# w_in cast to bf16 by the GpSimd queue's DMAs, VectorE's first step put in TensorE's order, and the last two blocks as whole-array matmuls

## The chip, the cores and the metric

The kernel runs on one core of one Trainium2 chip. The metric is the device time of one execution in microseconds (us). Nine executions of the kernel before gave a median of 699.18 us (698.62 to 701.48). Step and line numbers below are those of the kernel before; "u" is the index 0 to 15 of a tile of 128 columns of the hidden layer, "s" the index 0 to 31 of a step.

## The reference

`x` is [8, 4096, 192] float32. A causal convolution over the sequence with 7 taps comes first; the taps are the softmax of `weight` [8, 7] and each of the 8 heads owns 24 channels. The result, seen as 32768 tokens of 192 channels, goes through a feed-forward layer:

```python
h = x @ w_in                                  # [32768,192] @ [192,2048]
g = h * (1.0 / (1.0 + np.exp(-beta * h)))     # beta: one value for each of the 2048 columns
return (g @ w_out).astype(np.float32)         # [32768,2048] @ [2048,192]
```

## The kernel before, in words

The work is cut into 32 steps of 2 x 512 tokens: the same 512 positions of sequences p and p+4 (index h = 0, 1). The 192 channels are split as 64 partitions x 3 (index j or c), and the two values of h lie on partitions 0 to 63 and 64 to 127. So all of `w_in` is held twice as bf16, once on each half of the partitions (tile `w_in_s`, [128, 3, 2048]).

A step does this for each u:

- `hidden` (L405 to L424): six 64-row matmuls, three for each half, which run in pairs on the two halves of the array, into one of two PSUM buffers `ph`; then ScalarE's Silu (L421) from `ph` into `g`. It computes beta*h*sigmoid(beta*h), and `w_out` is divided by beta row by row in turn (`scale_w_out`, L305, four quarters on VectorE).
- `output` (L490): a number of "pairs". One pair is two 64-row matmuls of 192 columns (L443), on the two halves of the contraction, into the two rows of a PSUM tile `pa` or `pb`. A `Job` is two blocks of 128 tokens and takes 32 pairs; four jobs make a step's 128. When a job is done, `leave` (L454) adds the two rows on VectorE (L462) and SP stores the block. The last two jobs of the last step hold one block each (16 pairs); for those ScalarE copies one row (L459) and VectorE adds the other (L460). A job can take u only once u-2 of its own step is activated (LAG = 2), and steps 1 to 31 issue 8 pairs per u; step 0 issues 53 in all, so 75 pairs are always carried over into the next step.

The convolution of step s+2 is VectorE's work during step s and s+1: one multiply (L395) and six multiply-adds (L397) over [128, 1536] bf16, drawn from `queue`, one for each odd u (the "pops", L545). Its input is loaded two or three steps ahead (L95, SP), cast to bf16 (L106) and transposed by DMA (L127, SP).

The program writes out the order of every engine by hand (`manual_schedule`); each engine runs its own list in order. The start differs from a steady step:

- Step 0's tokens `x0` are cast (L241), transposed on TensorE (L248), copied by ScalarE (L290), and convolved on TensorE with seven diagonal matrices for each of c = 0, 1, 2 (L279). The three results leave PSUM by VectorE (L321, c = 0, 1) and ScalarE (L323, c = 2).
- `beta` is loaded by SP (L169) behind x0 and one half of w_in, and is transposed by a TensorE matmul (L331) that stands between the taps of c = 1 and those of c = 2.
- The first quarter of w_in (512 columns, u = 0 to 3) is loaded as float32 to both halves, one by SP (L168) and one by ScalarE's queue (L219), and cast by ScalarE (L301).
- Quarters 1 to 3 are cast by DMAs from GpSimd's queue (L208) to partitions 0 to 63 only; a small GpSimd copy (`hold`, L326) keeps them back until c = 0 is convolved. VectorE copies each to the other half (`copy_w_in`, L212, at u = 3, 5 and 9).
- Step 1's tokens `x1` are transposed on TensorE in `second` (u = 1 to 3). Its convolution is split: c = 0 on TensorE (`conv1`, taps 0 to 3 at u = 4 and 4 to 6 at u = 6, out of PSUM by VectorE, L381), c = 1, 2 on VectorE (seven operations over 1024 elements, L395 and L397, popped at u in 4, 6, 8, 9, 11, 12, 13).
- `fill` (L229) issues matmuls on zeros ahead of the first work.

SP issues its DMAs in this order: x0 (2), half of w_in's first quarter, beta, x1 (2), w_out (4), x of steps 2 and 3 (4), then transposes and stores.

Of the kernel before, what the change touches and what calls it, by code (L numbers as in the profile page):

```python
# [9 lines left out]
FP32 = mybir.dt.float32  # L10
FP32R = mybir.dt.float32r
BF16 = mybir.dt.bfloat16
AF = mybir.ActivationFunctionType
ALU = mybir.AluOpType
# [3 lines left out]
def kernel(  # L18
# [17 lines left out]
    nc = tc.nc  # L36

    B, S, D = x.shape
    H, K = weight.shape
    F = moe_w_in.shape[1]  # L40
    group = D // H
    DG = 64
    NG = D // DG
# [11 lines left out]
    N_ST = N_CH  # L55
# [6 lines left out]
    setup = ctx.enter_context(tc.tile_pool(name="setup", bufs=1))  # L62
# [70 lines left out]
    NW = 4  # L133
    FW = F // NW
# [3 lines left out]
    x0b = setup.tile([128, NB, NG, 2, DG], BF16)  # L138
    x1b = setup.tile([128, NB, NG, 2, DG], BF16)
    w_in_s = consts.tile([128, NG, F], BF16)  # L140
    w_in_raw = setup.tile([128, NG, FW], FP32)
    w_out_s = consts.tile([128, NF, D], BF16)
    w_out_raw = setup.tile([128, NF, D], FP32)
    w_in_v = moe_w_in.rearrange("(p c) f -> p c f", c=NG)
# [7 lines left out]
    cw8 = setup.tile([H, K], FP32)  # L152
    beta_q = setup.tile([NF, 128], FP32)
    nc.scalar.dma_start(out=cw8, in_=weight)


    def load_x(dst, t0):
# [7 lines left out]
            )  # L165

    load_x(x0, 0)
    nc.sync.dma_start(out=w_in_raw[0:DG], in_=w_in_v[:, :, 0:FW])  # L168
    nc.sync.dma_start(out=beta_q, in_=moe_beta.rearrange("(c p) -> c p", p=128))  # L169
    load_x(x1, TOK)  # L170
    for i in range(NW):
        load_w_out(i)
# [12 lines left out]
        out=sel,  # L185
        in_=sel,
# [7 lines left out]
        out=sel,  # L194
# [7 lines left out]
    ident = setup.tile([128, 128], FP32)  # L202
    make_identity(nc, ident)


    def load_w_in(i):
        cols = slice(i * FW, (i + 1) * FW)
        nc.gpsimd.dma_start(out=w_in_s[0:DG, :, cols], in_=w_in_v[:, :, cols])  # L208

    def copy_w_in(i):  # L210
        cols = slice(i * FW, (i + 1) * FW)
        nc.vector.tensor_copy(w_in_s[DG : 2 * DG, :, cols], w_in_s[0:DG, :, cols])  # L212

    nmax = setup.tile([H, 1], FP32)
    nc.vector.reduce_max(nmax, cw8, axis=mybir.AxisListType.X, negate=True)
    nc.scalar.activation(
        e8[:, 0:K], cw8, AF.Exp, bias=nmax, accum_out=e8[:, K : K + 1]
    )
    nc.scalar.dma_start(out=w_in_raw[DG : 2 * DG], in_=w_in_v[:, :, 0:FW])  # L219
    nc.scalar.activation(warm, warm, AF.Silu)  # L220
    sel_r = setup.tile([H, 2, DG], FP32R)
    nc.vector.tensor_copy(sel_r, sel)
# [75 lines left out]
    )  # L298
    rn = setup.tile([128, 1], FP32)
    nc.vector.reciprocal(rn, eu[:, K : K + 1])  # L300
    nc.scalar.copy(w_in_s[:, :, 0:FW], w_in_raw)  # L301
    beta = consts.tile([128, NF], FP32)
    beta_r = setup.tile([128, NF], FP32)

    def scale_w_out(i):  # L305
        fcs = slice(i * NQ, (i + 1) * NQ)
        nc.vector.tensor_tensor(  # L307
            w_out_s[:, fcs, :],
            w_out_raw[:, fcs, :],
            beta_r[:, fcs].unsqueeze(2).to_broadcast((128, NQ, D)),  # L310
            ALU.mult,
        )

    new_ct(0)
    for c in range(NG):
        pv = psum_h.tile([128, 2, TOK], FP32, name="ph") if c < 2 else in_a()
        pv = pv[:, 0, :]
        for k in range(K):
            diag_tap(k, xt0[:, c], pv)
        if c < 2:  # L320
            nc.vector.tensor_scalar_mul(cts[0][:, c, :], pv, rn)  # L321
        else:
            nc.scalar.mul(cts[0][:, c, :], pv, rn)  # L323
        if c == 0:
            hold = setup.tile([1, 1], BF16)
            nc.gpsimd.tensor_copy(hold, cts[0][0:1, 0, 0:1])  # L326
            for i in range(1, NW):
                load_w_in(i)
        if c == 1:
            pb = in_b()[:, 0, 0:NF]  # L330
            nc.tensor.transpose(pb, beta_q, ident[0:NF, 0:NF])  # L331
            nc.vector.tensor_copy(beta, pb)
            nc.vector.reciprocal(beta_r, beta)
            for b in range(NB):
                cast_rows(x1b, x1, b)
# [4 lines left out]
    def second():  # L340
        xt = new_xt(1)
        pt = in_b()
        halves = [
            pt[:, i, 0 : NG * BLK].bitcast(BF16).rearrange(
                "p (c b q) -> p c b q", c=NG, b=2
            )
            for i in range(2)
        ]
        for i in range(2):
            for b in range(2):  # L350
                transposes(halves[i][:, :, b], x1b, 2 * i + b)
            t = HALO + i * 2 * BLK
            nc.vector.tensor_copy(  # L353
                xt[:, :, t : t + 2 * BLK].rearrange("p c (q b) -> p c q b", b=2),
                halves[i].rearrange("p c b q -> p c q b"),
            )
            if i == 0:
                halo(1, xt0)
                scale_w_out(0)
            yield  # L360
        pq = pt[:, 0, NG * BLK : NG * BLK + K + 1]
        spread(pq, sel, e8)
        copy_w_in(1)
        rq = setup.tile([128, 1], FP32)
        nc.vector.reciprocal(rq, pq[:, K : K + 1])
        nc.vector.tensor_scalar_mul(cw, pq[:, 0:K], rq)
        yield
# [4 lines left out]
    def conv1():  # L372
        nc.vector.tensor_copy(
            xt1[:, HALO - PAD :], xts[1][:, 0, HALO - PAD :]
        )
        new_ct(1)
        pv = in_b()[:, 0, :]
        for k in range(K):
            diag_tap(k, xt1, pv)
            if k == K - 1:  # L380
                nc.vector.tensor_scalar_mul(cts[1][:, 0, :], pv, rn)  # L381
            if k in CONV1.values():
                yield
        yield

    def conv_ops(s, c0):
# [38 lines left out]

    class Job:
        def __init__(self, s, h, q, nb):
            self.s, self.h, self.q, self.nb = s, h, q, nb  # L430
            self.done, self.po = 0, None

        def ready(self, s, u):
# [3 lines left out]
        def pair(self):  # L437
            fc, b = divmod(self.done, self.nb)
            g = gs[self.s]
            q = self.q + b  # L440
            for r in range(2):
                rows = slice(r * 64, (r + 1) * 64)
                nc.tensor.matmul(  # L443
                    self.po[:, r, b * D : (b + 1) * D],
                    g[rows, fc, self.h, q * BLK : (q + 1) * BLK],
                    w_out_s[rows, fc, :],
                    start=(self.done == 0),
                    stop=(fc == NF - 1),
                    skip_group_check=True,
                )  # L450
            self.done += 1
            return self.done == NF * self.nb

        def leave(self):  # L454
            nb = self.nb
            osb = osb_pool.tile([128, 2, D], FP32, name="osb")
            dst = osb[:, 0:nb, :].rearrange("p b d -> p (b d)")
            if nb == 1:
                nc.scalar.copy(dst, self.po[:, 0, 0 : nb * D])  # L459
                nc.vector.tensor_tensor(dst, self.po[:, 1, 0 : nb * D], dst, ALU.add)  # L460
            else:
                nc.vector.tensor_reduce(  # L462
                    dst,
                    self.po[:, :, 0 : nb * D].rearrange("p r n -> p n r"),
                    axis=mybir.AxisListType.X,
                    op=ALU.add,
                )
            p, c = divmod(self.s, CHUNKS)
            t = c * TOK + self.q * BLK
            nc.sync.dma_start(  # L470
                out=out_v[self.h, p, t : t + nb * BLK, :].rearrange(
                    "(b q) d -> q b d", q=BLK
                ),
                in_=osb[:, 0:nb, :],
            )
# [14 lines left out]
    def output(s, u, pairs, free):  # L490
# [18 lines left out]
    second_work = second()  # L509
    conv1_work = conv1()  # L510
    first_work = {
        4: lambda: scale_w_out(1),
        5: lambda: copy_w_in(2),
        7: lambda: scale_w_out(2),
        9: lambda: copy_w_in(3),
        11: lambda: scale_w_out(3),
    }

    queue = deque()
    for s in range(N_ST):  # L520
        jobs_of(s)
        at = 8 if s == 0 else 0
        for u in range(NF):
            if s > 0 or u > 1:
                hidden(s, u)
            elif u == 0:
                phs = [hidden(0, fc, range(NG - 1)) for fc in range(2)]
                for fc in range(2):
                    hidden(0, fc, range(NG - 1, NG), phs[fc])
            if s == 0 and 0 < u < 4:  # L530
                next(second_work)
            if s == 0 and u in CONV1:
                next(conv1_work)
            if s > 0:
                output(s, u, 8, "ab")
            elif u > max(CONV1):
                output(s, u, 5, "ab")
            elif u > 2 and u not in CONV1:
                output(s, u, 4, "a")
            if s == 0 and u in first_work:  # L540
                first_work[u]()

            if s == 0 and u == min(CONV1):
                queue.extend(conv_ops(1, 1))
            pops = u % 2 if s > 0 else u in (4, 6, 8, 9, 11, 12, 13, 15)  # L545
            if pops and queue:
                queue.popleft()()

            if u == at and s + 3 < N_CH:
                load(s + 3)  # L550
            if u == at and s + 2 < N_CH:
                cast(s + 2, 0)
            if u == at + 1 and s + 2 < N_CH:
                cast(s + 2, 1)
                xpose(s + 2)
            if u == 12 and s + 2 < N_CH:
                queue.extend(conv_ops(s + 2, 0))
# [32 lines left out]
```

## Time and profile before

| | |
|---|---|
| median of 9 executions | 699.18 us |
| the profiled execution, its time | 698.97 us |
| its span, first to last instruction | 697.3 us |
| TensorE matmul busy | 686.9 us (99%) |
| ScalarE busy | 577.8 us (83%) |
| VectorE busy | 522.9 us (75%) |
| GpSimd busy | 3.5 us (1%) |
| DMA, mean share of 16 engines | q1 (SP) 34.7%, q0 (GpSimd) 0.5%, q10 (ScalarE) 0.2% |
| mean granted TensorE clock | 0.998 of full speed |
| first matmul of `hidden` | 13.89 us |
| last Silu begins | 685.72 us |
| last instruction of VectorE begins | 694.12 us |

All times in the profile count from the span's start. A row of the timeline reads: start, length, engine, line, operation, output <- input, shape, how many (x), and in brackets how long the engine sat idle before it and what it waited for. PEld is TensorE's weight load. A row of the windows view reads: window, its length, then for each engine the busy time and the number of instructions, the granted TensorE clock, the DMA share and GB/s. Matmul ends are modelled, and a row's length holds the latency of the last one; from the distance of two starts one reads the rate.

### The profile page before, as it was taken

To read this page: it belongs to the slowest core of one execution; us is meant where nothing else is said; L and a number is where in the kernel's file an instruction comes from. 1 tells how busy PE (TensorE), PEld (TensorE's weight loads), DVE (VectorE), ACT (ScalarE), POOL (GpSimd) and SP (SyncE) were. 2 spreads that over 40 slices of the span, in tenths; PEclk is the share of its full clock that TensorE was granted. 3 is DMA by queue.
4 is the path that set the end of the run, shared out by engine and by line. 5 is a ranking of instruction groups with operands and counts; after the bars stand their busy time and mean duration, and the time that the engine had idled before them with its cause. 6 is when DMAs were issued, how large, how long until landed. Compare 5 with 4: busy or idle time off the path is not lost.

```text
span 697.3 us, 24377 instructions
## 1 busy us (share of the span) xinstructions
PE 686.9 (99%) x11332; PEld 520.2 (75%) x11332; DVE 522.9 (75%) x472; ACT 577.8 (83%) x526; POOL 3.5 (1%) x13
## 2 busy tenths in 40 slices
PE   7999999999999999999999999999999999999997
PEld 4567777777777777777777777777777777777776
DVE  4888777977777977777977777977777977777722
ACT  5868888888888888888888888888888888888883
POOL 2000000000000000000000000000000000000000
PEclk9999999999999999999999999999999999999999
DMA  8543323433324433323433323543323434322111
GB/s 225 138 115 98 102 58 101 115 104 93 107 56 103 115 103 99 99 59 102 115 103 99 102 58 100 116 104 98 103 57 101 115 104 98 102 54 60 47 36 58
DMA packets 120821, 66.66 MB, mean 96 GB/s; under 512 B 53184, under 2 KB 120336, under 8 KB 120720
## 3 DMA queue, kind: packets, MB, share of 16 engines
q1 hardware_dynamic: 119872, 64.13, 34.7%
q8 instruction: 88, 1.44, 0.9%
q0 software_dynamic: 624, 0.59, 0.5%
q10 hardware_dynamic: 224, 0.39, 0.2%
q14 instruction: 13, 0.11, 0.1%
HBM read 28.71 MB, written 25.17 MB: 77 GB/s over the span
## 4 chain that ended last, share of the span: by engine, by line
PE 95%; DVE 2%; DMA 1%; issue 0%; SPq 0%; ACT 0%
PE ph L413 47%; PE pa L443 24%; PE pb L443 24%; DMA beta_q<-in_moe_beta_dram 1%; DVE ct L397 1%; DVE w_out_s L307 0%; PE pb L279 0%; PE pa L279 0%; DVE xb L106 0%; ACT g L421 0%; DVE osb L462 0%; DVE xt L353 0%; SPq L160 0%; DVE ct L381 0%; DVE w_in_s L212 0%
## 5 line engine op out<-in xcount | busy, mean ns | idle before, releaser
L421 ACT ACTIVATE g<-ph,beta 128x1024 bf16<-128x1024 f32 x512 | 569.9, 1114 | 102.2 <-PE ph L413 97.9
L443 PEld LDWEIGHTS <-g 64*128 64x128 bf16 x8192 | 369.6, 94 | 106.0 <-issue 1.4
L413 PE MATMUL ph<-ct,w_in_s 64*128 64x512 bf16 x3072 | 424.3, 377 | 2.5 <-DVE ct L397 2.0
L397 DVE SCALAR_TENSOR_TENSOR ct<-xt,cw,ct 128x1536 bf16<-128x1536 bf16 (+1 forms) x186 | 333.7, 1794 | 2.3
L443 PE MATMUL pa<-w_out_s,g 64*128 64x192 bf16 x4128 | 245.7, 243 | 0.9 <-DVE osb L462 0.5
L443 PE MATMUL pb<-w_out_s,g 64*128 64x192 bf16 x4064 | 237.1, 243 | 0.0
L413 PEld LDWEIGHTS <-w_in_s 64*128 64x128 bf16 x3072 | 157.9, 94 | 57.3 <-issue 3.8
L462 DVE TENSOR_REDUCE osb<-pa 128x384 f32<-128x768 f32 x64 | 61.2, 956 | 129.3 <-PE pa L443 129.3
L462 DVE TENSOR_REDUCE osb<-pb 128x384 f32<-128x768 f32 x63 | 60.1, 953 | 25.6 <-PE pb L443 25.6
L106 DVE CAST xb<-xf 128x768 bf16<-128x768 f32 x60 | 40.6, 678 | 0.0
L395 DVE TENSOR_SCALAR ct<-xt,cw 128x1536 bf16<-128x1536 bf16 (+1 forms) x31 | 30.7, 990 | 1.7 <-DMA xt<-xb 1.7
L231 PE MATMUL ph<-zeros 128*128 128x512 bf16 (+3 forms) x12 | 4.6, 482 | 1.3 <-DVE warm L178 1.3
L301 ACT CAST w_in_s<-w_in_raw 128x1536 bf16<-128x1536 f32 x1 | 1.5, 1472 | 4.7 <-DMA w_in_raw<-in_moe_w_in_dram 4.7
L459 ACT COPY osb<-pb 128x192 f32<-128x192 f32 x1 | 0.3, 319 | 5.6 <-PE pb L443 5.6
L121 DVE COPY xt<-xt 128x18 bf16<-128x18 bf16 x27 | 4.3, 160 | 0.0
L279 PE MATMUL ph<-xt,diag 128*128 128x512 f32 x14 | 3.5, 399 | 0.5 <-DVE rn L300 0.5
L307 DVE TENSOR_TENSOR w_out_s<-w_out_raw,beta_r 128x768 bf16<-128x768 f32 x4 | 3.8, 946 | 0.0
L321 DVE TENSOR_SCALAR ct<-ph,rn 128x512 bf16<-128x512 f32 x2 | 1.5, 752 | 2.8 <-PE ph L279 2.8
L279 PEld LDWEIGHTS ph<-xt,diag 128*128 128x128 f32 x14 | 2.5, 187 | 1.3 <-ACT xt L290 0.8
L353 DVE COPY xt<-pb 128x768 bf16<-128x768 bf16 x2 | 1.9, 958 | 1.3 <-PE pb L248 1.3
L231 PEld LDWEIGHTS <-zeros 128*128 128x128 bf16 x12 | 1.3, 125 | 2.1 <-DVE warm L178 1.3
L241 DVE CAST x0b<-x 128x384 bf16<-128x384 f32 x4 | 1.5, 413 | 1.4 <-DMA x<-in_x_dram 1.4
(58 smaller groups left out, 31.9 us busy)
## 6 DMA issues: line engine op xcount, KB each, us to landing
out_dram<-osb SPq DMA_DIRECT2D x127, 192.0 KB, 2.2
xf<-in_x_dram SPq DMA_DIRECT2D x60, 384.0 KB, 4.4
xt<-xb SPq DMA_TRANSPOSE x120, 2.8
x<-in_x_dram SPq DMA_DIRECT2D x4, 384.0 KB, 6.9
w_out_raw<-in_moe_w_out_dram SPq DMA_DIRECT2D x4, 384.0 KB, 11.3
w_in_s<-in_moe_w_in_dram POOLq DMA_DIRECT2D x3, 192.0 KB, 8.1
w_in_raw<-in_moe_w_in_dram SPq DMA_DIRECT2D x1, 384.0 KB, 9.6
w_in_raw<-in_moe_w_in_dram ACTq DMA_DIRECT2D x1, 384.0 KB, 9.6
```

What stands on the lines that cost most here:

```text
L106: nc.vector.tensor_copy(xbs[ch][:, :, :, h, :], xfs[ch][:, h].rearrange("q b (p c) -> q b c p", c=NG),)
L121: nc.vector.tensor_copy(dst, last[:, :, HALO + TOK - PAD :])
L231: nc.tensor.matmul(pf[:, 0, 0:cols], zeros[:, 0:128], zeros[:, 0:cols], start=True, stop=True)
L279: nc.tensor.matmul(pv, diag[:, k, :], xt[:, o : o + TOK], start=(k == 0), stop=(k == K - 1))
L307: nc.vector.tensor_tensor(w_out_s[:, fcs, :], w_out_raw[:, fcs, :], beta_r[:, fcs].unsqueeze(2).to_broadcast((128, NQ, D)), ALU.mult,)
L353: nc.vector.tensor_copy(xt[:, :, t : t + 2 * BLK].rearrange("p c (q b) -> p c q b", b=2), halves[i].rearrange("p c b q -> p c q b"),)
L395: nc.vector.tensor_scalar_mul(dst, src, scalar)
L397: nc.vector.scalar_tensor_tensor(out=dst, in0=src, scalar=scalar, in1=dst, op0=ALU.mult, op1=ALU.add)
L413: nc.tensor.matmul(ph[:, h, :], w_in_s[rows, j, fc * 128 : (fc + 1) * 128], cts[s][rows, j, :], start=(j == 0), stop=(j == NG - 1),)
L421: nc.scalar.activation(gs[s][:, fc], ph, AF.Silu, scale=beta[:, fc : fc + 1])
L443: nc.tensor.matmul(self.po[:, r, b * D : (b + 1) * D], g[rows, fc, self.h, q * BLK : (q + 1) * BLK], w_out_s[rows, fc, :], start=(self.don ...
L462: nc.vector.tensor_reduce(dst, self.po[:, :, 0 : nb * D].rearrange("p r n -> p n r"), axis=mybir.AxisListType.X, op=ALU.add,)
```

## The change

It has three parts.

1. All of w_in comes as bf16 from GpSimd's queue: eight DMAs, four quarters x two halves, issued first thing after GpSimd's setup. The float32 tile `w_in_raw`, its two loads, ScalarE's cast, the `hold` copy and VectorE's three copies go. `beta` is loaded from ScalarE's queue, directly behind `weight` and ahead of ScalarE's first table load.
2. Step 0: VectorE's eviction of `conv1` (L381) moves from u = 6 to u = 8; `scale_w_out(1)` from u = 4 to 5, `scale_w_out(2)` from u = 7 to 8; the pops are at u in 4, 6, 7, 9, 11, 12, 13; the load and the two casts of step 2's x move from u = 8, 9 to 9, 10. Output goes on at 4 pairs, slot "a" only, through u = 8 (before: 5 pairs on both slots from u = 7). Twelve pairs of step 0 are put ahead of the first `hidden` of step 1.
3. The end: the last step issues 7 pairs per u instead of 8, and the last two one-block jobs use one 128-row matmul per u instead of a pair, so that ScalarE's copy alone empties them.

The instruction lists show: step 0 has 51 pairs and then the 12; step 1 has 8 pairs per u up to u = 13, then 7 and 4; step 2 starts as before with 8 for each u; after the last `hidden` and its 7 pairs there are 56 pairs and the 32 whole-array matmuls (before: 8 pairs, then 43 pairs and the 32 pairs of the one-block jobs).

```diff
-    w_in_raw = setup.tile([128, NG, FW], FP32)
+    nc.scalar.dma_start(out=beta_q, in_=moe_beta.rearrange("(c p) -> c p", p=128))
...
-    nc.sync.dma_start(out=w_in_raw[0:DG], in_=w_in_v[:, :, 0:FW])
-    nc.sync.dma_start(out=beta_q, in_=moe_beta.rearrange("(c p) -> c p", p=128))
...
+    for i in range(NW):
         cols = slice(i * FW, (i + 1) * FW)
-        nc.vector.tensor_copy(w_in_s[DG : 2 * DG, :, cols], w_in_s[0:DG, :, cols])
+        for r in range(2):
+            nc.gpsimd.dma_start(
+                out=w_in_s[r * DG : (r + 1) * DG, :, cols], in_=w_in_v[:, :, cols]
+            )
...
-    nc.scalar.dma_start(out=w_in_raw[DG : 2 * DG], in_=w_in_v[:, :, 0:FW])
-    nc.scalar.copy(w_in_s[:, :, 0:FW], w_in_raw)
...
-            hold = setup.tile([1, 1], BF16)
-            nc.gpsimd.tensor_copy(hold, cts[0][0:1, 0, 0:1])
-            for i in range(1, NW):
-                load_w_in(i)
...
-            if k == K - 1:
-                nc.vector.tensor_scalar_mul(cts[1][:, 0, :], pv, rn)
             if k in CONV1.values():
                 yield
+        nc.vector.tensor_scalar_mul(cts[1][:, 0, :], pv, rn)
         yield
...
+            self.nr = 2 if nb > 1 else 1
...
-            for r in range(2):
-                rows = slice(r * 64, (r + 1) * 64)
+            n = 128 // self.nr
+            for r in range(self.nr):
+                rows = slice(r * n, (r + 1) * n)
...
-                nc.scalar.copy(dst, self.po[:, 0, 0 : nb * D])
-                nc.vector.tensor_tensor(dst, self.po[:, 1, 0 : nb * D], dst, ALU.add)
+                nc.scalar.copy(dst, self.po[:, 0, 0:D])
...
-        4: lambda: scale_w_out(1),
-        5: lambda: copy_w_in(2),
-        7: lambda: scale_w_out(2),
-        9: lambda: copy_w_in(3),
+        5: lambda: scale_w_out(1),
+        8: lambda: (next(conv1_work), scale_w_out(2)),
         11: lambda: scale_w_out(3),
...
-        at = 8 if s == 0 else 0
+        at = 9 if s == 0 else 0
         for u in range(NF):
+            if s == 1 and u == 0:
+                output(s, u, 12, "ab")
...
-                output(s, u, 8, "ab")
-            elif u > max(CONV1):
+                output(s, u, 8 if s < N_ST - 1 else 7, "ab")
+            elif u > 8:
                 output(s, u, 5, "ab")
...
-            pops = u % 2 if s > 0 else u in (4, 6, 8, 9, 11, 12, 13, 15)
+            pops = u % 2 if s > 0 else u in (4, 6, 7, 9, 11, 12, 13)
```

More of the change, by code (lines that the diff above doesn't have):

```diff
@@ L203 @@
     make_identity(nc, ident)
-    def load_w_in(i):
+    for i in range(NW):
         cols = slice(i * FW, (i + 1) * FW)
-        nc.gpsimd.dma_start(out=w_in_s[0:DG, :, cols], in_=w_in_v[:, :, cols])
-    def copy_w_in(i):
-        cols = slice(i * FW, (i + 1) * FW)
-        nc.vector.tensor_copy(w_in_s[DG : 2 * DG, :, cols], w_in_s[0:DG, :, cols])
+        for r in range(2):
+            nc.gpsimd.dma_start(
+                out=w_in_s[r * DG : (r + 1) * DG, :, cols], in_=w_in_v[:, :, cols]
+            )
     nmax = setup.tile([H, 1], FP32)
@@ L323 @@
             nc.scalar.mul(cts[0][:, c, :], pv, rn)
-        if c == 0:
-            hold = setup.tile([1, 1], BF16)
-            nc.gpsimd.tensor_copy(hold, cts[0][0:1, 0, 0:1])
-            for i in range(1, NW):
-                load_w_in(i)
         if c == 1:
@@ L362, in second @@
         spread(pq, sel, e8)
-        copy_w_in(1)
         rq = setup.tile([128, 1], FP32)
```

## The prediction

> **What bounds the kernel now.** I read the page's busy shares and chain of waits first, then the windows and the timeline of both ends.
>
> ```profile
> PE 686.9 (99%) x11332; PEld 520.2 (75%) x11332; DVE 522.9 (75%) x472; ACT 577.8 (83%) x526; POOL 3.5 (1%) x13
> ...
> PE 95%; DVE 2%; DMA 1%; issue 0%; SPq 0%; ACT 0%
> ```
>
> TensorE (PE) carries 95% of the chain. Steady `hidden` starts lie 1.307 us apart (61.17, 62.48 in the timeline), a step takes 20.92 us, and the change leaves that work as it is: `hidden` 0.64 us and 8 pairs at 0.082 us. So only TensorE's lost time at the two ends can move. Four places lose it.
>
> ```profile
> 11.94 0.20 PE L331 MATMUL pb<-ident,beta_q 16*128 16x16 f32 x1 [0.93 <-DMA beta_q<-in_moe_beta_dram]
> 12.07 1.89 PE L279 MATMUL pa<-xt,diag 128*128 128x512 f32 x7
> 12.06 1.47 ACT L301 CAST w_in_s<-w_in_raw 128x1536 bf16<-128x1536 f32 x1 [4.68 <-DMA w_in_raw<-in_moe_w_in_dram]
> 13.89 0.98 PEld L413 LDWEIGHTS <-w_in_s 64*128 64x128 bf16 x12 [0.35 <-ACT w_in_s L301]
> ```
>
> Start: the transpose of beta waits 0.93 us for its DMA in front of the last seven taps; w_in's cast ends at 13.53, near their end.
>
> ```profile
> 33.80 0.40 PE L413 MATMUL ph<-ct,w_in_s 64*128 64x512 bf16 x2
> 36.17 0.69 PE L413 MATMUL ph<-ct,w_in_s 64*128 64x512 bf16 x4 [1.97 <-DVE ct L397]
> 36.62 0.88 PE L443 MATMUL pa<-w_out_s,g 64*128 64x192 bf16 x8
> 37.26 0.88 PE L443 MATMUL pb<-w_out_s,g 64*128 64x192 bf16 x8
> 37.90 1.52 PE L413 MATMUL ph<-ct,w_in_s 64*128 64x512 bf16 x6
> ```
>
> First step boundary: step 1's first `hidden` stands until VectorE (DVE) has convolved step 1. Then every matmul takes twice its length; the next row is the windows view's, with the clock granted (its tenth figure).
>
> ```profile
> 35.00:40.00 5.00, 3.83 (x36) 2.77 (x37) 3.29 (x4) 1.65 (x2) 0.00 (x0) 0.66 0.20 41
> ```
>
> Clock 0.66 over 5 us is about 3.4 us at half speed, 1.7 us of work lost.
>
> ```profile
> 686.88 0.34 PE L443 MATMUL pa<-w_out_s,g 64*128 64x192 bf16 x4 [0.38 <-ACT g L421]
> ...
> 688.28 2.82 PE L443 MATMUL pa<-w_out_s,g 64*128 64x192 bf16 x64 [0.48 <-DVE osb L462]
> ...
> 692.23 1.50 PE L443 MATMUL pa<-w_out_s,g 64*128 64x192 bf16 x32
> 693.77 0.32 ACT L459 COPY osb<-pa 128x192 f32<-128x192 f32 x1 [1.00 <-PE pa L443]
> 694.12 0.36 DVE L460 TENSOR_TENSOR osb<-pa,osb 128x192 f32<-128x192 f32 x1 [0.96 <-ACT osb L459]
> ```
>
> End: a wait for the last Silu, one for a VectorE reduce, and after the last matmul a ScalarE copy and a VectorE add in line.
>
> **The start.** With beta early, its transpose follows the taps of c = 1 (end 11.01) and the last taps start at 11.20, not 12.07: 0.87 us. ScalarE's result of c = 2 and all behind it (first Silu at 15.19) move with them, if w_in's first quarter is on both halves by 13.1, when those taps end. The old cast hides nowhere any more, so the DMA decides.
>
> No GpSimd DMA started this early before. The nearest rows: three issued from 10.36 (0.67 us each), first packets 3.7 us later, landed 7.4, 8.1 and 9.1 us after their issues, while SP's queue was full, too. The first quarter is now the first two of eight, issued at 2.24 and 2.9: the second lands at 2.9 + 8.1 = 11.0. Bounds: like x0's first half into an empty queue (3.3 us), 6.2; like the float32 quarter (9.6 us), 12.5. I take 11.0, the row of the same kind; cover 2 us. Later quarters at the measured 1.5 us per DMA land near 14, 17 and 20; they are wanted at 18.4, 24 and 28.
>
> x0 is not disturbed: it lands at 5.55 and GpSimd's packets start near 6. Between 15 and 18 us GpSimd's queue moved 134 packets per us and SP's about 130 beside it. At that pace x1 (no longer behind w_in) lands near 9 instead of 13.8, w_out's first quarter near 12.5 (wanted 15.8), step 2's x near 23 (wanted 26). All hidden, by 1 to 3 us.
>
> The price: beta's issue (0.58 us on SP) now stands on ScalarE ahead of its first table load (1.45). The Exp result, the `spread` matmul (3.51) and two fills move by as much; the fills still run at half rate (starts 0.427 us apart for 512 columns). The first x0 transposes go from 4.59 to about 5.1, ScalarE's four copies end at about 7.57 instead of 7.38, and the taps start 0.15 late. Bounds: 0, and 1.7 us should the clock rise one 3.4-us stretch later. I take 0.15. Start: +0.87 - 0.15 = 0.72.
>
> **Step 0 and the boundary.** VectorE loses three copies (3 x 0.684 = 2.05 us) and, with the eviction at u = 8, its 1.99 us wait for `conv1`'s taps. From rows: xt copy ends 17.7; reciprocal, scale, cast 1.0; first tap 0.48; `scale_w_out` 0.95; two taps 2.5; eviction 0.75 (its taps end at 23.1); scale 0.95; tap 1.25; two casts and halo 1.45; scale 0.95; three taps 3.8. Sum: step 1's convolution ends near 32.3, not 36.1.
>
> TensorE keeps its old pace to u = 7, as in the trace (24.0 becomes 23.2), then ScalarE sets it at 1.09 us per Silu (nine in 9.86). Silu 15 starts near 32.8 (before 33.62) and ends at 33.9. The 12 extra pairs stand in front of `hidden`: two run, two wait for that Silu, a new stall of about 1.0 us with all of step 1 queued behind it; then 10 pairs, 0.82 us, and `hidden` starts at 34.8, long after its input. Its u = 2 starts at 37.4, with 79 pairs done; before at 40.25, with 69. For ten pairs (0.82 us): 40.25 + 0.82 - 37.4 = 3.67 us gained, the 0.72 included.
>
> This takes the half clock as gone. The case for it: 10 to 15 us held 0.93 us of idle time like the new one, busy 4.07 of 5, at clock 1.00. If not, 1.7 us come back.
>
> The Trainium skill ("TensorE: Matmul & The Clock Gate", "HAM oscillation") asks for idle gaps above some 3.4 us for that drop; this trace drops after 1.97 us, so the measurement decides, and by the rule alone the new stall would be safe by still more.
>
> Step 1 can't take 8 pairs in u = 14, 15 (7 and 4). Step 2's second pair group then asks for Silu 15 at 1.77 us after its `hidden`, and it ends at 2.03: 0.25 us lost once. VectorE's convolution of step 2 ends near 52.5 and is wanted at 55.4: hidden. Later steps are as before.
>
> **The end.** The last step's pairs move behind it, equal work. The wait for Silu stays (0.66 by starts: 7 pairs cover less; before 0.56). The one for the reduce goes (0.66: 687.62 to 688.28), since 20 pairs, 1.64 us, now lie between, and the reduce takes 0.96. The add and its gap go: 0.39. Sum before the matmuls themselves: 0.56 + 0.39 = 0.95.
>
> Whole-array matmuls of 192 columns are in no row. The nearest: x1b's transposes, 128 columns, weights changed each time, start 58 ns apart; times 1.5 that is 87 at most, against 82 for a pair. If the weight load (57 ns) were not hidden, 32 x 57 = 1.8 us more. I take equal time, since the transposes hide theirs. Going from half to whole array between `hidden` and taps left gaps of 0.1 to 0.3 us; one switch, 0.2. End: 0.95 - 0.2 = 0.75.
>
> **Sum:** 3.67 - 0.25 + 0.75 = 4.17 us off the profiled execution's 698.97 (span 697.3), so 694.8. The median of nine runs is 0.21 higher; I forecast 694.9.
>
> The skill's page "DMA: Bandwidth & Descriptors" ("Rules for kernel authors") speaks against loading two partition halves separately, as they serialize on the same engines. In this trace the three one-half DMAs took 5 us from first packet to last beside SP's; by the rule eight would need about 13 us as an estimate, and the deadlines above allow that, so it would leave the sum as it is.
>
> **Rivals.**
>
> *The clock stays low somewhere* (after the 1.0 us stall at 33, or a later rise at the start): 1.7 us, so 696.5. For: one such drop after 2 us. Against: none after 0.93. Chance 0.17. The whole-array matmuls with an open weight load (696.7) fall in with it: 0.05.
>
> *Part of the first quarter is late* without undoing all: it lands at 14 to 17, `hidden` waits 1 to 4 us; 697.8 to 699. For: ScalarE's half quarter took 9.6 us behind SP's backlog. Chance 0.06.
>
> *The eight DMAs run side by side, not in order.* If their descriptors share the engines equally, the first quarter lands with the last, near 20 us, instead of 11. `hidden` waits at 13.1 for 6.9 us, against 4.1 gained: 701.7, slower. It decides from a landing at 17.3 on. For: x1, w_in and beta, issued within 2 us, all landed within 11.4 to 13.8. Against: the three earlier DMAs landed 1.3 to 1.7 us apart, in order. Chance 0.09.
>
> *The change does nothing at the boundary*: if VectorE's order were held up elsewhere (step 2's x late at u = 9), step 1's convolution would end near 36 again; the gain would be start and end alone, 1.5 us: 697.4. Chance 0.03.
>
> **Numbers.** Forecast 0.60. About 0.2% (1.4 us) can be told from no change. Faster by more: 0.60 + 0.17 + 0.05 + 0.03 = 0.85, less 0.02 for mishaps that add up: 0.83; within: 0.07; slower: 0.10. The range's low end has no late taps, no stall in step 2 and no switch: 694.9 - 0.6 = 694.3, and 0.5 for run to run: 693.8. The high end takes in the clock and the weight load, and one of them beside some lateness: 698.0.
>
> **What would show it.** Right: beta's transpose near 11.2; no idle time before the first `hidden`; no VectorE copy of w_in; a wait of about 1 us for Silu near 33 and none for L397's convolution; clock 1.00 from 30 to 40; no wait for a reduce at the end, and ScalarE's copy last. Wrong: TensorE waiting for w_in's DMA near 13, clock under 1 after 33, or whole-array matmuls starting over 100 ns apart.

## The result and the profile after

The changed kernel takes **701.58 us** (median of 10 runs, 701.33 to 702.77) against 699.19 us (31 runs of the kernel before): a ratio of 1.0032 [1.0023, 1.0041]. It is slower, by 0.3%, where 0.6% faster was forecast. The profiled execution took 701.72 us, with a span of 699.9 us. From here each kernel's rows bear its own line numbers; in the changed kernel `hidden` is L400, the Silu L408, a pair's matmul L433 and the VectorE reduce L451.

The page of the kernel after, busy shares and the chain of waits by engine and by line:

```profile
PE 691.1 (99%) x11300; PEld 517.5 (74%) x11300; DVE 519.6 (74%) x467; ACT 576.1 (82%) x525; POOL 6.5 (1%) x17
...
PE 92%; DVE 4%; ACT 2%; issue 1%; ACTq 0%
PE ph L400 44%; PE pa L433 25%; PE pb L433 22%; DVE osb L451 4%; ACT g L408 2%; PE ph L274 1%; PE pb L274 0%; PE pa L274 0%; PE pb L243 0%; PE ph L226 0%; ACT xt L285 0%; DVE xt L342 0%; DVE w_out_s L301 0%; ACTq L153 0%; ACT L177 0%
```

TensorE has 32 matmuls fewer and is yet busy 4.2 us longer, still "99%". The busy row hides what happened; the chain shows it. VectorE's reduce L451 now holds 4% of the chain (28 us), and TensorE has gone from 95% to 92%.

The timeline of the kernel after, at the two ends and the first step boundary (columns as before):

```profile
11.19 0.23 PE L320 MATMUL pb<-ident,beta_q 16*128 16x16 f32 x1
...
11.36 1.89 PE L274 MATMUL pa<-xt,diag 128*128 128x512 f32 x7
...
13.17 1.47 PE L400 MATMUL ph<-ct,w_in_s 64*128 64x512 bf16 x12
...
33.52 0.34 PE L433 MATMUL pa<-w_out_s,g 64*128 64x192 bf16 x4 [0.63 <-ACT g L408]
...
34.36 0.81 PE L400 MATMUL ph<-ct,w_in_s 64*128 64x512 bf16 x6
...
689.58 0.34 PE L433 MATMUL pa<-w_out_s,g 64*128 64x192 bf16 x4 [0.46 <-ACT g L408]
...
691.41 2.80 PE L433 MATMUL pa<-w_out_s,g 64*128 64x192 bf16 x64
...
694.14 1.49 PE L433 MATMUL pb<-w_out_s,g 128*128 128x192 bf16 x16
...
697.00 0.32 ACT L449 COPY osb<-pa 128x192 f32<-128x192 f32 x1 [1.00 <-PE pa L433]
```

These places went as forecast. The transpose of beta waits for nothing, `hidden` starts at 13.17 (before 13.89) without a wait for w_in, the boundary has a wait of 0.63 us for the Silu in place of 1.97 for the convolution, and at the end the wait for the reduce and VectorE's add are gone. The windows view of the kernel after shows a full clock (1.00) behind the boundary:

```profile
35.00:40.00 5.00, 5.00 (x88) 3.71 (x86) 4.54 (x6) 4.21 (x4) 0.00 (x0) 1.00 0.59 169
```

**Where the time went.** The first reduce of `pa` in step 2 starts at 56.29 us, before at 59.75: 3.46 us ahead, and three pairs (0.25 us) further with the work. From there the kernel loses. By the distance of the same reduce from step to step (77.46, 98.62 us), a step takes 21.17 us; before it took 20.92 (59.75, 80.67). The timeline of the kernel after, where a step begins:

```profile
76.91 0.51 PE L433 MATMUL pa<-w_out_s,g 64*128 64x192 bf16 x8
...
77.24 0.51 PE L433 MATMUL pb<-w_out_s,g 64*128 64x192 bf16 x8
77.46 0.96 DVE L451 TENSOR_REDUCE osb<-pa 128x384 f32<-128x768 f32 x1 [2.81 <-PE pa L433]
...
77.57 0.83 PE L400 MATMUL ph<-ct,w_in_s 64*128 64x512 bf16 x6
...
78.47 0.83 PE L433 MATMUL pa<-w_out_s,g 64*128 64x192 bf16 x16
78.47 0.60 PEld L433 LDWEIGHTS <-g 64*128 64x128 bf16 x15 [0.37 <-issue]
```

The same place in the timeline of the kernel before:

```profile
59.21 0.51 PE L443 MATMUL pa<-w_out_s,g 64*128 64x192 bf16 x8
59.48 2.36 ACT L421 ACTIVATE g<-ph,beta 128x1024 bf16<-128x1024 f32 x2 [0.25 <-PE ph L413]
59.54 0.51 PE L443 MATMUL pb<-w_out_s,g 64*128 64x192 bf16 x8
59.75 0.96 DVE L462 TENSOR_REDUCE osb<-pa 128x384 f32<-128x768 f32 x1 [1.92 <-PE pa L443]
...
59.87 0.82 PE L413 MATMUL ph<-ct,w_in_s 64*128 64x512 bf16 x6
...
60.51 0.42 PE L443 MATMUL pb<-w_out_s,g 64*128 64x192 bf16 x6
...
60.76 0.59 PE L443 MATMUL pa<-w_out_s,g 64*128 64x192 bf16 x10
```

At u = 0 the job in slot "a" is done, and VectorE must empty `pa` before the next job may write it. From the start of the matmuls behind the last `pa` pair to the end of the reduce lie 1.2 us in both (77.24 to 78.42, 59.54 to 60.71). Before, 8 `pb` matmuls (0.33 us), a `hidden` (0.64) and 6 more `pb` matmuls (0.25) fill it, 1.22 us, and `pa` goes on at 60.76 with no wait. After, the 6 are missing: `hidden` has issued its work by 77.57 + 0.65 = 78.22 and `pa` starts at 78.47, 0.25 us late. The waits view of the kernel after, from 40 to 690 us, counts these (columns: who waited <- for whom: us in total, times, longest):

```profile
PEld L433 <- issue: 11.0, 30, 0.4
```

Once for each of steps 2 to 31. No engine is named: the matmul waits for `pa`, the weight loads behind it wait with it, and the view calls this "issue". In the kernel before the same view has one such wait, at the very end (688.28), and none in the steps:

```profile
PEld L443 <- issue: 0.6, 1, 0.6
```

Why the six are missing: a job may take u only once u-2 is activated (LAG), so at the end of a step each of the two live jobs has at most 28 of its 32 pairs done. The least that can be carried into the next step is thus 4 + 4 + 64 = 72 pairs. The kernel before carries 75 (4 in slot "a", 7 in "b"). After, step 1 is offered more than it may take, and ends at that floor: 72, four and four. Both jobs then end at u = 0, and nothing is left to stand between the two jobs of slot "a". Every later step issues 128 pairs for 128, so the state of step 1's end is handed on to step 31.

### The profile page after: what moved, and what is told of

It reads as the page before. It is cut to its first block, busy times and chain, and to the rows that moved or that the text cites. A ratio compares the mean times of both kernels' runs of the same rounds, so it can differ in the third digit from the quotient of the medians.

```text
span 699.9 us, 24308 instructions
## 1 busy us (share of the span) xinstructions
PE 691.1 (99%) x11300; PEld 517.5 (74%) x11300; DVE 519.6 (74%) x467; ACT 576.1 (82%) x525; POOL 6.5 (1%) x17
## 4 chain that ended last, share of the span: by engine, by line
PE 92%; DVE 4%; ACT 2%; issue 1%; ACTq 0%
PE ph L400 44%; PE pa L433 25%; PE pb L433 22%; DVE osb L451 4%; ACT g L408 2%; PE ph L274 1%; PE pb L274 0%; PE pa L274 0%; PE pb L243 0%; PE ph L226 0%; ACT xt L285 0%; DVE xt L342 0%; DVE w_out_s L301 0%; ACTq L153 0%; ACT L177 0%
## 5 line engine op out<-in xcount | busy, mean ns | idle before, releaser
L408 ACT ACTIVATE g<-ph,beta 128x1024 bf16<-128x1024 f32 x512 | 569.7, 1114 | 105.9 <-PE ph L400 100.4
L433 PEld LDWEIGHTS <-g 64*128 64x128 bf16 x8160 | 366.8, 94 | 115.2 <-issue 11.1
L400 PE MATMUL ph<-ct,w_in_s 64*128 64x512 bf16 x3072 | 422.5, 376 | 0.6 <-ACT g L408 0.6
L433 PE MATMUL pa<-w_out_s,g 64*128 64x192 bf16 x4112 | 239.7, 243 | 3.3 <-ACT g L408 1.1
L433 PE MATMUL pb<-w_out_s,g 64*128 64x192 bf16 (+1 forms) x4048 | 225.1, 243 | 0.0
L400 PEld LDWEIGHTS <-w_in_s 64*128 64x128 bf16 x3072 | 156.4, 94 | 55.5 <-issue 1.8
L451 DVE TENSOR_REDUCE osb<-pa 128x384 f32<-128x768 f32 x64 | 61.2, 957 | 154.8 <-PE pa L433 154.8
L451 DVE TENSOR_REDUCE osb<-pb 128x384 f32<-128x768 f32 x63 | 60.1, 953 | 9.2 <-PE pb L433 7.6
L206 POOL DMA_DIRECT2D w_in_s<-in_moe_w_in_dram x8 | 5.1, 646 | 0.0
## 6 DMA issues: line engine op xcount, KB each, us to landing
w_in_s<-in_moe_w_in_dram POOLq DMA_DIRECT2D x8, 192.0 KB, 11.4
```

The source lines that it names most:

```text
L206: nc.gpsimd.dma_start(out=w_in_s[r * DG : (r + 1) * DG, :, cols], in_=w_in_v[:, :, cols])
L400: nc.tensor.matmul(ph[:, h, :], w_in_s[rows, j, fc * 128 : (fc + 1) * 128], cts[s][rows, j, :], start=(j == 0), stop=(j == NG - 1),)
L408: nc.scalar.activation(gs[s][:, fc], ph, AF.Silu, scale=beta[:, fc : fc + 1])
L433: nc.tensor.matmul(self.po[:, r, b * D : (b + 1) * D], g[rows, fc, self.h, q * BLK : (q + 1) * BLK], w_out_s[rows, fc, :], start=(self.don ...
L451: nc.vector.tensor_reduce(dst, self.po[:, :, 0 : nb * D].rearrange("p r n -> p n r"), axis=mybir.AxisListType.X, op=ALU.add,)
```

## The experiments

The theory: the carried pairs alone, 72 for 75, cost 0.245 us in each of 30 steps, 7.4 us, and all else of the change wins what was forecast or a little more. The rival: the loss comes from another part of the change (the whole-array matmuls, the new order, the DMAs), and the carry goes with it by chance.

**e1_carry75**: the changed kernel, with step 1 stopped from reaching the floor.

```diff
-                output(s, u, 8 if s < N_ST - 1 else 7, "ab")
+                output(s, u, 7 if s == N_ST - 1 or (s == 1 and u >= 8) else 8, "ab")
```

> The changed kernel with one number more: step 1 issues 7 output pairs per u from u = 8 on, so 75 pairs are carried into each later step, as in the kernel before, not 72. Theory 'carry' (with 72, both slots' jobs end at u = 0, and slot a's next job, first thing at u = 1, waits for VectorE's reduce of the old one: 0.245 us in each of about 30 steps): 701.6 - 30 x 0.245 = 694.3, near the forecast. Rival 'state of the stream' (the loss in the steady steps comes from other things that the change shifted, VectorE's order, stores or transposes, not from where the jobs end): 701.6 as before it, step 21.17 us.

Measured: 693.99 us, ratio to the kernel before 0.9923 [0.9908, 0.9937]. A row of its waits view from 40 to 690 us, and the begin of a step in its timeline:

```profile
PEld L433 <- issue: 0.2, 1, 0.2
...
76.49 0.96 DVE L451 TENSOR_REDUCE osb<-pa 128x384 f32<-128x768 f32 x1 [1.92 <-PE pa L433]
...
77.27 0.41 PE L433 MATMUL pb<-w_out_s,g 64*128 64x192 bf16 x6
...
77.51 0.58 PE L433 MATMUL pa<-w_out_s,g 64*128 64x192 bf16 x10
```

The six `pb` matmuls stand between the two jobs again, the step is back at 20.92 us (the next such reduce is at 97.41), and the 30 waits are gone; the one that is left stands at the end (686.27). The whole loss, 7.6 us, hangs on three pairs that step 2 issues instead of step 1.

**e2_before_carry72**: the kernel before, with three pairs more in step 0 and nothing else of the change.

```diff
-                output(s, u, 5, "ab")
+                output(s, u, 8 if u == NF - 1 else 5, "ab")
```

> The kernel before with one number changed: 8 pairs instead of 5 at the last u of step 0, so that 72 pairs are carried instead of 75; nothing else of the change. Theory 'carry': each step longer by 0.245 us, 30 x 0.245 = 7.3, so 706.5, with a steady step of 21.17 us. Rival 'state of the stream': 699.2, step 20.92.

Measured: 706.58 us, 1.0103 [1.0088, 1.0118]. Its waits view from 40 to 690 us has the 30 waits:

```profile
PEld L443 <- issue: 11.2, 30, 0.4
```

The old kernel takes the same loss when it carries 72 (step 21.17 us: reduces at 80.79 and 101.96), so neither the DMAs, nor VectorE's order, nor the end is needed for it. The rival falls.

**e3_carry74** and **e4_carry78**: the changed kernel with 7 pairs from u = 9 or from u = 5 of step 1. They ask how the loss depends on the count.

```diff
-                output(s, u, 8 if s < N_ST - 1 else 7, "ab")
+                output(s, u, 7 if s == N_ST - 1 or (s == 1 and u >= 9) else 8, "ab")
```

> The changed kernel with 74 pairs carried (7 pairs per u in step 1 from u = 9 on). Theory 'carry': a pair covers 0.082 us of the wait, so two of the three pairs' worth is covered: 30 x 0.08 = 2.4 us lost, 696.7. Rival 'state of the stream': 701.6. A third, 'all or nothing' (the loss comes from both jobs ending in the same u, not from a wait that is covered pair by pair): 694.3.

> after with 78 pairs carried from step to step (7 pairs per u in step 1 from u = 5 on). Theory: the three pairs that 75 leave in slot b already cover VectorE's reduce (1.23 us of other work against 1.23 needed), so three more bring nothing per step: 694.0, as e1_carry75 (693.99). Rival: the cover at 75 is still short by something in each step, so that more pairs go on winning; 0.05 us a step would give 692.5.

Measured: 74 pairs 696.54 us, 0.9962 [0.9947, 0.9977]; 78 pairs 693.86 us, 0.9922 [0.9907, 0.9936].

| pairs carried | work between the jobs of slot "a", us | step, us | kernel |
|---|---|---|---|
| 72 | 0.98 | 21.17 | after, e2_before_carry72 |
| 74 | 0.98 + 2 x 0.082 = 1.14 | 21.00 | e3_carry74 |
| 75 | 0.98 + 3 x 0.082 = 1.22 | 20.92 | before, e1_carry75 |
| 78 | 1.47 | 20.92 | e4_carry78 |

Each pair buys 0.08 us a step, until 75 covers the reduce to within 0.01 us, and then nothing. The old kernel stood right at the edge.

**e5_half_reduce**: the changed kernel, carry 72, with a shorter VectorE instruction in the place of the reduce: a copy of one of the two rows, which leaves out half of each sum.

```diff
-                nc.vector.tensor_reduce(
-                    dst,
-                    self.po[:, :, 0 : nb * D].rearrange("p r n -> p n r"),
...
+                nc.vector.tensor_copy(dst, self.po[:, 0, 0 : nb * D])
```

> The changed kernel with 72 pairs carried, but VectorE copies one of the two rows of a finished job instead of adding both (half of the contraction is left out of those blocks); that reads half as much. Theory 'carry': the copy takes about 0.5 us instead of 0.96, the wait at u = 1 goes: 694.3. Rival 'Silu' (slot a waits at u = 0 for the last Silu of the step, and this wait is the loss, whatever the reduce takes): 701.6.

Measured: 694.95 us (694.42 to 695.56), 0.9934 [0.9918, 0.9951]. Its timeline at a step's begin:

```profile
78.27 0.56 DVE L451 COPY osb<-pa 128x384 f32<-128x384 f32 x1 [3.22 <-PE pa L433]
...
78.40 0.81 PE L400 MATMUL ph<-ct,w_in_s 64*128 64x512 bf16 x6
79.05 0.82 PE L433 MATMUL pa<-w_out_s,g 64*128 64x192 bf16 x16
```

The copy is over at 78.83, while the `hidden` still issues, and `pa` follows 0.65 us after that one's start, on time. At 72 pairs it is the reduce's length, then, that costs. The median is 0.65 us above what was expected: two of the four runs took 694.42 and 694.44 us, two 695.46 and 695.56. In the profiled one, of the longer two, this is the start: the fourteen taps of c = 0 and 1 took 4.67 us, in the changed kernel 3.78, and the first `hidden` came at 14.24 instead of 13.17. The last section has the reason.

**e6_w_in_only**: the kernel before with part 1 alone (w_in by GpSimd's queue to both halves, beta early, the casts and copies gone).

```diff
-        nc.gpsimd.dma_start(out=w_in_s[0:DG, :, cols], in_=w_in_v[:, :, cols])
+        for r in range(2):
+            nc.gpsimd.dma_start(
+                out=w_in_s[r * DG : (r + 1) * DG, :, cols], in_=w_in_v[:, :, cols]
+            )
```

> The kernel before with the first part alone: w_in by eight cast DMAs to both halves, beta on ScalarE's queue, no float32 tile, no ScalarE cast, no VectorE copies; VectorE's order, the pacing of output and the end as before, 75 pairs carried. Theory 'DMAs are in time and hidden': the start gains 0.7, VectorE's convolution of step 1 ends near 34 instead of 36.1, the wait at the first boundary shrinks to under 1 us and the half clock goes (1.7 us): 699.1 - 3.9 = 695.2. Rival 'the DMAs cost': the eight transfers delay x1, w_out or step 2's x, and the gain stays under 2 us: above 697.

Measured: 696.91 us, 0.9970 [0.9958, 0.9982], less of a gain than expected. Its timeline at the boundary tells why:

```profile
34.10 0.61 PE L402 MATMUL ph<-ct,w_in_s 64*128 64x512 bf16 x4 [1.39 <-DVE ct L386]
...
35.66 1.01 DVE L384 TENSOR_SCALAR ct<-xt,cw 128x1536 bf16<-128x1536 bf16 x1 [1.62 <-DMA xt<-xb]
...
37.59 0.59 PE L432 MATMUL pa<-w_out_s,g 64*128 64x192 bf16 x10 [1.33 <-DVE osb L451]
```

`hidden` still waits for the convolution, since VectorE still stood 2.81 us for `conv1`'s taps (eviction at 22.88). A second wait comes behind it: the pop of u = 15 stands on VectorE for the transposes' DMA, with the reduce of `pa` queued behind it, and TensorE waits for that reduce. By the reduce of step 2 (57.50 against 59.75) part 1 alone wins 2.25 us; the changed kernel had 3.71 there (3.46 and the three pairs). So part 2 as a whole (VectorE's order, the pacing of output and the twelve pairs) is worth 1.46 us of it, or 1.8 us if one allows for the first `hidden`, which was 0.32 us earlier in e6 (12.85 against 13.17).

The expectation counted the half clock as 1.7 us to be won, and most of the shortfall lies there: the second wait, 1.33 us, came in its place. In the profiled execution of e2, the kernel before but for three pairs, the clock stayed full at this boundary, and the second wait stands there too; a row of the windows view and one of the timeline:

```profile
35.00:40.00 5.00, 2.45 (x40) 1.73 (x41) 3.30 (x4) 2.23 (x2) 0.00 (x0) 1.00 0.20 41
...
39.47 0.84 PE L443 MATMUL pa<-w_out_s,g 64*128 64x192 bf16 x16 [1.66 <-DVE osb L462]
```

(Three pairs more in between would leave 1.4 us of it.) In the kernel before itself, at half clock, the same `pa` comes 0.05 us behind the end of that reduce, so a full clock could hardly have brought it earlier:

```profile
38.75 0.95 DVE L462 TENSOR_REDUCE osb<-pa 128x384 f32<-128x768 f32 x1
...
39.75 0.68 PE L443 MATMUL pa<-w_out_s,g 64*128 64x192 bf16 x10
```

So in the old order most of the half clock's 1.7 us lies over a wait for VectorE that comes at full clock instead. What the changed kernel wins there goes with VectorE being done earlier.

**e7_end_only**: the kernel before with part 3 alone.

```diff
-                nc.scalar.copy(dst, self.po[:, 0, 0 : nb * D])
-                nc.vector.tensor_tensor(dst, self.po[:, 1, 0 : nb * D], dst, ALU.add)
+                nc.scalar.copy(dst, self.po[:, 0, 0:D])
```

> The kernel before with the third part alone: 7 pairs per u in the last step, whole-array matmuls for the last two blocks, ScalarE's copy alone behind them; 75 pairs carried. Theory: the wait for the reduce (0.66) and the add (0.39) go, the wait for the last Silu grows by 0.1, one switch costs 0.1: 699.1 - 0.85 = 698.25. Rival 'equal': whole-array matmuls or the switch cost what the add saved, 698.7 to 699.1.

Measured: 698.57 us (12 runs, 697.83 to 700.7), 0.9995 [0.9985, 1.0004]: not settled by the times. The profile has it: from the last `hidden` to the end of the last instruction 10.00 us (683.59 to 693.59) with 15 more pairs behind it, 1.23 us, against 9.63 (684.85 to 694.48) before: 0.86 us won. In the changed kernel the same sum (687.55 to 697.32, 12 more pairs, 0.98 us) gives 0.84.

**e8_extra_after**: e1_carry75, with the twelve extra pairs not ahead of step 1's first `hidden`, but four each behind its u = 1, 2 and 3. It tests the forecast stall at 33 us, and is the version that the runs point to.

```diff
-            if s == 1 and u == 0:
-                output(s, u, 12, "ab")
...
+                n_out = 7 if s == N_ST - 1 or (s == 1 and u >= 8) else 8
+                output(s, u, 12 if s == 1 and 0 < u < 4 else n_out, "ab")
```

> The version with 75 pairs carried, with the 12 extra pairs of step 0 put behind step 1's first hidden (4 more at each of u = 1, 2, 3) instead of ahead of it. Theory: the wait for the last Silu of step 0 (0.63 us idle, 0.85 by the weight load) had all of step 1 queued behind it; hidden now fills it: 694.0 - 0.7 = 693.3. Rival: the wait only moves behind the hidden, or step 1's convolution (ready near 32.0) is now late: 694.0.

Measured: **693.04 us** (692.95 to 693.49), 0.9913 [0.9900, 0.9926], the fastest here. The wait of 0.63 us for the Silu is gone, and `hidden` of step 1 starts at 32.50 instead of 34.36:

```profile
32.50 0.83 PE L400 MATMUL ph<-ct,w_in_s 64*128 64x512 bf16 x6
```

The median is 0.95 us below that of e1. Of this the profiled executions show 0.47 by step 2's reduce (55.10 against 55.57), although e8's first `hidden` was 0.21 us later there (13.12 against 12.91): 0.68 us for the place of the twelve pairs, 0.7 forecast. The rest is not located.

**e9_beta_sp** and **e10_beta_later**: e8 with beta's load moved off the head of ScalarE's queue, to SP between x0 and x1, or on ScalarE to behind its first Exp. They test the price put on that issue.

```diff
-    nc.scalar.dma_start(out=beta_q, in_=moe_beta.rearrange("(c p) -> c p", p=128))
...
     load_x(x0, 0)
+    nc.sync.dma_start(out=beta_q, in_=moe_beta.rearrange("(c p) -> c p", p=128))
```

> As the version with the 12 pairs behind hidden, with beta loaded by SP between x0 and x1 instead of by ScalarE's queue. Theory: ScalarE's first table load starts 0.34 us earlier, the spread matmul and the fills with it, and the taps of c = 0 lose less to the half clock: 0.2 to 0.3 us, 693.05. Rival: x0's landing sets the taps, and beta's place is worth nothing: 693.3.

> e8_extra_after (693.04) with the load of beta still on ScalarE's queue, but issued behind ScalarE's first Exp table load instead of ahead of it (where the kernel before issued w_in's second half). Theory: the issue (0.34 us in the profile of after) leaves the path from weight to the taps, so the Exp result is back at about 3.25 us (before) instead of 3.63, the taps start near 7.2 as in e9_beta_sp, the first hidden near 12.65 instead of 13.12, and x1 and w_out are as early as in e8, since SP's queue is not touched: 692.6 (693.04 - 0.45). beta is needed at about 10.7 us and should land near 8. Rival: x0's landing sets the start, since it was there at 5.3 us and the 14 taps alone ran 0.3 us slower in e8; then the time is that of e8, 693.0. A late beta (a wait in front of the last seven taps) would give 693.0 to 694.

Measured: e9 694.23 us, 0.9936 [0.9923, 0.9948]; e10 693.08 us, 0.9911 [0.9896, 0.9927], no better than e8. Two rows of e9's timeline, a row of its windows view, and a row of e10's timeline:

```profile
17.06 0.96 DVE L301 TENSOR_TENSOR w_out_s<-w_out_raw,beta_r 128x768 bf16<-128x768 f32 x1 [1.45 <-DMA w_out_raw<-in_moe_w_out_dram]
...
18.94 0.38 PE L231 MATMUL pb<-e,sel 8*128 8x8 f32 x2 [1.84 <-DVE xt L342]
```

```profile
20.00:25.00 5.00, 5.00 (x29) 2.34 (x26) 3.96 (x5) 2.26 (x3) 0.00 (x0) 0.67 1.11 328
```

```profile
5.48 0.85 DVE L236 CAST x0b<-x 128x384 bf16<-128x384 f32 x2 [0.27 <-DMA x<-in_x_dram]
```

In e9 the taps start at 7.19 (e8: 7.48; x0's two halves had also landed 0.16 and 0.11 us earlier than there), but everything behind beta on SP's queue comes later: VectorE waits 1.45 us for w_out, TensorE 1.84 for VectorE. In e10 the Exp result is as early as in e9, and the taps still start at 7.49, because x0's second half lands 0.16 us later than in e8 (its cast 5.48, there 5.32). In this execution, then, x0's landing sets the start. The medians of e8 and e10 agree (693.04 and 693.08), as the rival of that run said: the issue costs nothing that the time shows. What it costs when x0 lands early is not shown.

## Why the prediction was wrong

**The step that failed** is the sentence "Later steps are as before". The prediction had just found that step 1 can't take all its pairs (7 and 4 in u = 14, 15), and priced that at one Silu wait, 0.25 us once. It did not ask in what state this leaves the two slots. Reaching the limit means that the carry is at its floor, 72, and the trace of before showed what the three missing pairs do: the six `pb` matmuls at 60.51, between a reduce that ends at 60.71 and the `pa` that starts at 60.76. e1, e2, e3 and e5 show that this is the cause; none of the rivals named it. With the terms measured: -3.71 (start and boundary) - 0.84 (end) + 30 x 0.247 = +2.86 us, where 0.247 us is the step's growth over steps 2 to 30 (from the reduce at 56.29 to the one at 648.96, before from 59.75 to 645.51); the profiled executions differ by 701.72 - 698.97 = +2.75.

**The other steps**, all against the changed kernel's trace:

- Start: 0.72 forecast, 0.72 measured (13.89 to 13.17). That the two agree is luck. The price of 0.15 was for taps that start late, and they did not (7.48, before 7.52); but the fourteen for c = 0, 1 took 3.78 us instead of 3.49, since the full clock came at 8.05 us in this execution and at 5.85 in the one before (last section). With the same order of DMAs the first `hidden` came at 12.85 in e6, 12.91 in e1 and 14.24 in e5.
- The eight DMAs landed 8.2, 11.4 and 14.7 us (least, median, most) after their issues, and TensorE waited for none: the order held, and the rival "side by side" fell. One reading of mine was off: the three DMAs before took 6.1 us from first packet to last (14.01 to 20.11), not 5, and the eight took 15.2 (5.68 to 20.89), not 13.
- Boundary: the eviction's order let VectorE end step 1's convolution at 31.99 (forecast 32.3). The Silu wait was 0.63 us (forecast 1.0), the clock stayed up, `hidden` started at 34.36 (34.8). The 1.7 us that I read as lost to the half clock were not a loss of their own (see e6); the forecast did not rest on them, since it compared the old trace's times with a new sequence. To step 2's reduce this gave 3.71 us, forecast 3.67 - 0.25 = 3.42; step 2's Silu wait was 0.29.
- My count of step 0 was off by two: it issues 49 pairs before the twelve, not 51, which put two pairs, 0.16 us, too much into the forecast gain.
- End: 0.84, forecast 0.75. Whole-array matmuls start 83 to 84 ns apart (694.14 to 695.48 for 16), a pair 82: equal, as taken. The switch cost 0.10 us, not 0.2.

So forecast and gain agree within a few tenths of a us where the change works (in part by luck, as said), and with the carry kept (e1) the time is 693.99, 0.9 us below the forecast (whose own sum, 694.8 + 0.21, gives 695.0): by the reduce of step 2 (55.57 against 59.75) e1 wins 4.18 us where 3.42 was forecast, 0.29 of it since its step 2 has no Silu wait and 0.26 by an earlier start, and at the end 0.85 instead of 0.75.

## What to carry to other kernels

In a software pipeline that hands unfinished work from step to step, the amount carried is a parameter of every later step: when a prologue is changed, count what it leaves in each slot, and compare the slot's time to come free with the work that stands between its two uses. Look in the trace of before for covers that just suffice (here 0.05 us between the end of a reduce and the matmul that needs it, as much as where the matmul waits: 78.42 to 78.47 after), since a gain at one end can take them away in each of 30 steps. A wait for a buffer may be booked as "issue" of the weight load while the matmul row stays at 99%; the chain and the step's length show it.

## What the runs showed of the hardware

- The granted clock fell to half after a TensorE wait of 1.84 us (e9, window 20 to 25 at 0.67) as it had after 1.97 us before, and not in e2 after waits of 1.72 and 1.66 us with 1.9 us of work between, nor in e6 after 1.39 and 1.33 us with 2.2 us between (both 1.00 from 30 to 40). The Trainium skill ("TensorE: Matmul & The Clock Gate", "HAM oscillation") asks for gaps above about 3.4 us; in these two traces less was enough. In the three traces with such a drop (before, e7, e9) the half clock lasted 3.41 us, and the full clock ahead of it a whole multiple of that (30.72 us, 9 times, in before and e7; 13.65 us, 4 times, in e9).
- The price of a drop depends on what stands behind it. Of e9's six runs two, the profiled one among them, were granted 0.998 over the span and took 695.92 and 695.77 us, four were granted 1.00 and took 693.97 to 694.30: about 1.7 us, as the prediction worked out for one stretch at half speed. Of the 18 executions of the kernel before that ran beside e9, seven were granted 1.00, with a median of 698.70 us, and eight 0.998, with 699.18 (three less): only 0.5 us, and the drop is not certain there.
- The clock rises at another moment in each execution. The trace's record of the granted clock begins, at full clock, at 5.85 us (before), 5.87 (e10), 7.97 (e8), 8.05 (after) and 10.25 (e5); the same fourteen taps took 3.49, 3.49, 3.73, 3.78 and 4.67 us. In e5 the taps start 0.43 us apart up to that moment and 0.23 behind it; in the changed kernel only the first two are far apart, 0.59 us, before 0.31. The windows view prints 1.00 for the stretch ahead of it too, where the trace has no record: a 1.00 there does not show a full clock.
- Between the last half-array matmul and the first whole-array one TensorE lost 0.10 us. The Trainium skill ("TensorEngine Tiling (Array Packing)", "Key Properties") says that a change of the tiling mode drains TensorE, without a size; 0.10 us is what such a change cost here.
